# Twelve loads for a head pair instead of seventeen, the scale on the queries, and a new order for every engine

## The chip, the cores and the metric

The kernel runs on one core of a Trainium2 chip. The metric is the time of one execution on the device, in microseconds (us).

## The reference

Two attention stages follow each other; all numbers are float32.

```python
# stage 1: q, k, v are [8 batches, 8 heads, 576 tokens, 64]
scores = q @ k.T / 8
keep   = scores >= max(scores, axis=-1) - tau          # tau = 0.02
attn   = exp(where(keep, scores, -1e9) - max) ; attn /= sum(attn) + 1e-9
x      = heads side by side of (attn @ v)              # [8, 576, 512]
# stage 2: four experts e of width 64, the two best of a token by its gate logits
logits = x @ w_gate                                    # [512, 4]
q, k, v = x @ wq[e], x @ wk[e], x @ wv[e]
ye     = softmax(causal(q @ k.T / 8)) @ v @ wo[e]
out   += (share of e in the token's two best) * ye     # [8, 576, 512]
```

## The kernel before

The work of stage 1 is cut into 32 **pairs**: two heads of one batch, numbered n. Pair n loads its queries, keys and values, turns queries and keys by TensorE transposes (tasks `tq.n`, `tk.n`), moves the turned tiles from PSUM to SBUF (the pairs 0 to 3 as plain float32, the later ones split into a high and a low part), and then makes five score tiles of 128 tokens or 64 (`scores`, tiles in the order 4, 2, 3, 0, 1). A score tile of one head costs VectorE two passes over 128x576: `s_min`, which moves the scores and finds the largest, and `s_stt`, which sets the threshold and sums. ScalarE makes the exponential between the two. A scaling by the reciprocal (`scale2`) may run on GpSimd, VectorE or ScalarE. Then TensorE transposes the weights (`turned`) and multiplies them with the values (`attnv`, the matmuls `pm`, `pt`, `pe` times `vm`, `vt`). After each fourth pair the second stage of that batch (`second`) follows: projections, gate, causal scores, values, output, store. Weights are split once into high and low parts at the start (`weights`).

All of it is a list of some 5,000 tasks. Nothing is scheduled on the chip: the table `ORDER` gives each task its place in one overall sequence, and the table `BY` gives the engine of each task that more than one engine can do. `plan` walks through the sequence with a cost for each task; from these costs it picks the PSUM banks and SBUF slots, and puts fillers (matmuls on `tri` whose result nobody reads) into the start. Each engine then runs its own tasks in the order in which they stand, and waits at each for what it needs. SyncE (SP) issues the loads and stores in its order too: a load that waits for its buffer holds up those behind it.

`ki` and `qi`, the tiles into which keys and queries are loaded, exist once (`SLOTS`), so a pair's keys can only be loaded when the transposes of the pair ahead have read them; `vm` and `vt` exist twice. For a pair the kernel issues 17 loads: six for the keys (`KEYS`), five for the queries (`QUERIES`), two of 128 KB for the values and four for the last 64 tokens of the values (`vt`). Every piece of keys or values is one token's row of 64 numbers, 256 bytes. The keys are scaled by -1/8 (`qsc`, made from `tau`) as they leave PSUM.

GpSimd and VectorE share a path to SBUF. `plan` held two lists of spans (`mine`, `theirs`) from which the function `hit` works out an expected delay, and `told` puts each GpSimd task behind the last VectorE pass of this kind.

Of the kernel before, what the change touches and what calls it, by code (L numbers as in the profile page):

```python
# [44 lines left out]
KEYS = tuple((j, *x) for j in range(2) for x in ((SM, 1, 0, 0), (0, 4, 1, 0), (WH - ST, 5, 0, 1)))  # L45
# [57 lines left out]
JIT = 50.0  # L103
# [7 lines left out]
class Space:  # L111
# [47 lines left out]

def plan(tasks, filler, told=None):  # L160
# [6 lines left out]
    mine, theirs, holder = [], [], None  # L167
    order = []
    for t in sorted(tasks, key=lambda t: t.place):
# [30 lines left out]
        if t.port and e == "DVE":  # L200
            more = sum(hit(start, a, z - 200.0) for a, z in theirs[-6:])
            mine.append((start, start + more + lat - 177.0))
            at["POOL"] += sum(hit(a, *mine[-1]) for a, z in theirs[-6:] if a > start)
        elif e == "POOL":
            more = sum(hit(start, a, z) for a, z in mine[-8:])
            theirs.append((start + more, start + more + lat))
            at["DVE"] += sum(hit(a, theirs[-1][0], theirs[-1][1] - 200.0) for a, z in mine[-8:] if a > start)
# [45 lines left out]
SMALL = (172, 80)  # L253


def work(K):
# [20 lines left out]
    def dma(fn, deps, takes=(), uses=(), move=576.0, name="", e="SP"):  # L277
        late = 0.0 if isinstance(e, str) else 500.0
# [41 lines left out]
    def load(n):  # L320
        ki, qi, vm = (Buf(x) for x in ("ki", "qi", "vm"))
        e = "SP" if n else ("SP", "ACT")
        into = lambda *a: (lambda: K.load_in(*a)) if n else lambda e: K.load_in(*a, e)
        dk = [dma(into(K.kis, K.k, n, *x, ki), (), [ki], move=72.0 * x[2], name=f"ldk.{n}", e=e) for x in KEYS]
        dq = [dma(into(K.qis, K.q, n, *x, qi), (), [qi], move=72.0 * x[2], name=f"ldq.{n}", e=e) for x in QUERIES]
        dv = [dma(lambda j=j: K.load_v(n, vm, j), (), [vm], name=f"ldv.{n}") for j in range(2)]
        dv += [dma(lambda j=j, x=x: K.load_vt(n, vm, j, x), (), [vm], move=72.0, name=f"ldv.{n}") for j in range(2) for x in range(2)]
# [3 lines left out]
    def prep(n):  # L331
        ki, qi, dk, dq, dv = LD[n]
        PREP[n] = []
        for cls, src, tiles, d, scale, f in (("kk", ki, K.kis, dk, True, "k"), ("qq", qi, K.qis, dq, False, "q")):
            buf, g = Buf(cls), Buf("d")
            if not n:
                o = []
                for y in range(2):
                    m = pe((R + 1) * TR + TX, lambda g=g, src=src, tiles=tiles, y=y: K.tr_in(g, tiles, src, (y,)), [z for z, a in zip(d, KEYS if scale else QUERIES) if a[-1] == y], [g], [src], "R", ld=76.0, kind="T", name=f"t{f}.{n}")
# [23 lines left out]
    def scores(n, s):  # L363
# [13 lines left out]
        ms = [task("DVE", (782, 80), lambda j=j: K.s_min(bufs[j], scs[j], sm, j), [a], [sc, sm], [bufs[j], sc, sm], name=f"min.{n}.{s}") for j in range(nj)]  # L377
# [4 lines left out]
        for j in range(nj):  # L382
            x = task("DVE", (831, 77), lambda j=j: K.s_stt(scs[j], sm, ees[j], j), [es[j], th], [], [sc, sm, ee], name=f"stt.{n}.{s}")
# [34 lines left out]
    def weights(c):  # L418
# [7 lines left out]
        gb = Buf("sm")  # L426
        d = dma(lambda: K.load_g(c, gb), (), [gb], move=72.0, name="w")
        h = task("POOL", (204, 30), lambda: K.g_hi(c, gb), [d], [], [gb], name="w")
        WT.append(task("POOL", (206, 30), lambda: K.g_lo(c, gb), [h], [], [gb], name="w"))
# [132 lines left out]
    TAU.append(dma(K.load_tau, (), move=8.0, name="tau", e=("SP", "ACT")))  # L562
# [4 lines left out]
    for n in range(NPR):  # L567
        load(n)
        prep(n)
# [29 lines left out]
    "ldk": [
# [8 lines left out]
    ],  # L608
    "ldq": [
# [7 lines left out]
    ],  # L617
    "ldv": [
# [1023 lines left out]
```

## Time and profile before

| what | value |
|---|---|
| median of three runs | 799.91 us (798.96 to 800.9) |
| the profiled execution, own time | 800.27 us |
| span of its instructions | 798.5 us |
| TensorE busy | 774.9 us (97% of the span) |
| VectorE busy | 714.1 us (89%) |
| ScalarE busy | 680.3 us (85%) |
| GpSimd busy | 378.2 us (47%) |
| granted TensorE clock | 1.0 of full speed |

The span runs from the first instruction to the last; the execution's own time is 1.77 us more. Matmuls overlap in TensorE, so a busy share of 97% says that there was nearly always one in flight, not that none waited.

### The profile page before, as it was taken

How to read it: one execution, taken by the hardware profiler on the slowest of the kernel's cores; microseconds unless marked ns; L12 is line 12 of the kernel's file. 1: busy time of each engine (PE TensorE's matmuls, PEld its weight loads, DVE VectorE, ACT ScalarE, POOL GpSimd, SP SyncE). 2: the span in 40 equal slices, each digit the busy share in tenths (PEclk: the TensorE clock that was granted, in tenths of full speed). 3: DMA queues.
4: the chain of work that ended last, by engine and by line, in shares of the span. 5: the costliest groups of instructions: out<-in, count | busy, mean ns of one | idle time of the engine just before them, and what ended most of it. 6: DMA issues, size and time to landing. Idle time of an engine off the chain costs nothing.

```text
span 798.5 us, 34332 instructions
## 1 busy us (share of the span) xinstructions
PE 774.9 (97%) x14047; PEld 724.3 (91%) x14047; DVE 714.1 (89%) x2271; ACT 680.3 (85%) x1294; POOL 378.2 (47%) x766
## 2 busy tenths in 40 slices
PE   9889999999999999999999999999999999999997
PEld 6677998899989999898999999999998999988997
DVE  6999989998999889999999988999999989999483
ACT  5999989988899789887899869999789987999474
POOL 3577445434554435634466435464264623456231
PEclk9999999999999999999999999999999999999999
DMA  4343211122122122222121222213222122210002
GB/s 112 82 90 87 60 36 29 45 51 73 36 67 71 35 54 55 50 65 68 41 73 35 70 70 50 47 23 75 54 47 52 42 73 66 56 31 12 9 28 95
DMA packets 140237, 44.19 MB, mean 55 GB/s; under 512 B 135216, under 2 KB 135216, under 8 KB 140080
## 3 DMA queue, kind: packets, MB, share of 16 engines
q1 hardware_dynamic: 138640, 41.65, 21.4%
q8 instruction: 111, 1.82, 1.0%
q10 hardware_dynamic: 1440, 0.34, 0.2%
q14 instruction: 46, 0.38, 0.2%
HBM read 32.51 MB, written 9.44 MB: 53 GB/s over the span
## 4 chain that ended last, share of the span: by engine, by line
PE 72%; DVE 11%; ACT 8%; SPq 3%; issue 2%; DMA 2%; POOL 1%; ACTq 0%; DVEq 0%
PE ps L1142 59%; PE ps L1276 10%; DVE e L992 8%; SPq L1145 3%; PE ps L1132 3%; ACT pm L1118 2%; ACT e L1255 2%; DMA qi<-in_q_dram 1%; ACT e L1530 1%; POOL e L992 1%; DVE sm L992 1%; ACT pt L1118 1%; ACT e L1551 0%; DVE z L992 0%; DMA ki<-in_k_dram 0%
## 5 line engine op out<-in xcount | busy, mean ns | idle before, releaser
L992 POOL TENSOR_SCALAR e<-e,sm 128x576 f32<-128x576 f32 (+4 forms) x289 | 196.1, 688 | 94.7 <-DVE sm L992 51.6
L992 DVE TENSOR_SCALAR_CACHE_REDUCE e<-ps 128x576 f32<-128x576 f32 x288 | 209.1, 751 | 19.1 <-PE ps L1142 12.9
L1255 ACT ACTIVATE e<-e,sm 128x576 f32<-128x576 f32 x288 | 212.5, 770 | 8.2 <-DVE e L992 7.4
L992 DVE SCALAR_TENSOR_TENSOR e<-e,sm,e 128x576 f32<-128x576 f32 x256 | 205.6, 828 | 7.2 <-POOL sm L992 2.7
L1142 PE MATMUL ps<-kk,qq 64*128 64x288 f32 x1840 | 175.0, 313 | 3.6 <-DVE e L992 1.0
L1142 PEld LDWEIGHTS ps<-kk,qq 64*128 64x128 f32 x1840 | 136.9, 185 | 15.5 <-DVE e L992 3.2
L1118 ACT ACTIVATE pm<-ps 128x1024 f32<-128x1024 f32 (+1 forms) x142 | 140.4, 1002 | 6.9 <-PE ps L1276 5.0
L1142 PE MATMUL ps<-pm,vm 128*64 128x128 f32 x2048 | 120.1, 273 | 0.0
L1276 PE MATMUL ps<-ident,e 64*128 64x64 f32 x2624 | 114.1, 225 | 5.8 <-POOL e L992 1.3
L1276 PEld LDWEIGHTS ps<-ident,e 64*128 64x128 f32 x2624 | 102.6, 138 | 15.1 <-POOL e L992 3.5
L1142 PEld LDWEIGHTS ps<-pm,vm 128*64 128x64 f32 x2048 | 111.1, 137 | 1.2 <-ACT pm L1118 0.4
L1142 PE MATMUL ps<-x,wh 64*128 64x288 f32 x1024 | 106.5, 294 | 0.0
L992 POOL TENSOR_TENSOR sm<-sm 128x2 f32<-128x2 f32 (+1 forms) x132 | 26.7, 208 | 137.7 <-DVE e L992 108.1
L1142 PEld LDWEIGHTS ps<-x,wh 64*128 64x128 f32 x1024 | 88.9, 185 | 0.3 <-issue 0.2
L1551 ACT ACTIVATE e<-e,sm 128x576 f32<-128x576 f32 (+4 forms) x113 | 80.2, 726 | 6.6 <-DVE sm L992 6.2
L1142 PE MATMUL ps<-x,wl 64*128 64x288 f32 x512 | 83.5, 292 | 0.0
L1530 ACT ACTIVATE e<-e,sm 128x384 f32<-128x384 f32 (+3 forms) x128 | 70.6, 555 | 4.8 <-DVE sm L992 4.6
L1142 PE MATMUL ps<-wh,x 64*128 64x260 f32 x576 | 60.5, 282 | 0.0
L992 DVE CUSTOM_DVE_ANT_0 e<-ps,tri 128x384 f32<-128x384 f32 (+3 forms) x128 | 58.6, 484 | 1.9 <-PE ps L1142 1.0
L1142 PE MATMUL ps<-woh,z 64*128 64x256 f32 x512 | 57.9, 289 | 1.1 <-DVE zt L992 0.4
L1142 PEld LDWEIGHTS ps<-x,wl 64*128 64x128 f32 x512 | 56.8, 184 | 0.0
L1118 ACT ACTIVATE rw<-ps 128x576 f32<-128x576 f32 (+1 forms) x57 | 36.8, 646 | 22.9 <-PE ps L1142 17.5
(151 smaller groups left out, 1498.2 us busy)
## 6 DMA issues: line engine op xcount, KB each, us to landing
vm<-in_v_dram SPq DMA_DIRECT2D x64, 128.0 KB, 2.5
out_dram<-ob SPq DMA_DIRECT2D x32, 256.0 KB, 2.2
ki<-in_k_dram SPq DMA_DIRECT2D x63, 80.0 KB, 2.4
qi<-in_q_dram SPq DMA_DIRECT2D x62, 80.0 KB, 2.4
ki<-in_k_dram SPq DMA_DIRECT2D x63, 64.0 KB, 2.3
qi<-in_q_dram SPq DMA_DIRECT2D x32, 64.0 KB, 2.3
vt<-in_v_dram SPq DMA_DIRECT2D x128, 16.0 KB, 2.2
qi<-in_q_dram SPq DMA_DIRECT2D x32, 48.0 KB, 2.4
```

The source lines that it names most:

```text
L992: self.made.append(f(*args, **kw))
L1118: self.nc.scalar.activation(dst, src, AF.Copy)
L1132: self.nc.tensor.transpose(self.ps[:, bank, c * n:(c + 1) * n], x[sl], self.ident[sl, sl])
L1142: return self.nc.tensor.matmul(out, x, y, start=first, stop=last)
L1145: (self.nc.sync if e == "SP" else self.nc.scalar).dma_start(dst, src)
L1255: self.nc.scalar.activation(self.row(e), self.row(sc), AF.Exp, bias=self.small(sm)[:, 2 * j:2 * j + 1], scale=-1.0)
L1276: self.nc.tensor.transpose(self.ps[:, g.slot + h, c * D:(c + 1) * D], x, self.ident[sl, sl])
L1530: self.nc.scalar.activation(p, p, AF.Exp, bias=m[:, 2 * j:2 * j + 1], scale=-1.0, accum_out=m[:, 4 + 2 * j:5 + 2 * j])
L1551: self.nc.scalar.activation(p, p, AF.Copy, scale=x)
```

## The change

A pair's keys arrive with two transfers of 128 KB, one for each head, in which every partition gets four tokens that lie one behind the other (1 KB), and two transfers of 16 KB each for half of the tile that holds the last 64 tokens of both heads. The values arrive the same way with one transfer of 256 KB for both heads, and their last 64 tokens with two transfers instead of four. The queries keep their five. The order of the keys within a head thereby changes, for keys and values alike. The scale moves from the keys to the queries: keys are copied out of PSUM, in pieces of 64 columns, and queries are multiplied by `qsc`. The gate's weights come in one transfer instead of four, with two GpSimd tasks instead of eight. The weights' loads wait for those of pair 0. In `plan` the expected delay on the shared path is replaced by a plain rule (a VectorE pass of this kind starts when GpSimd is done), and three VectorE costs are lowered. `ORDER` and `BY` are written anew.

```diff
-KEYS = tuple((j, *x) for j in range(2) for x in ((SM, 1, 0, 0), (0, 4, 1, 0), (WH - ST, 5, 0, 1)))
+KEYS = tuple((x, tail) for tail in range(2) for x in range(2))
...
         if t.port and e == "DVE":
-            more = sum(hit(start, a, z - 200.0) for a, z in theirs[-6:])
-            mine.append((start, start + more + lat - 177.0))
-            at["POOL"] += sum(hit(a, *mine[-1]) for a, z in theirs[-6:] if a > start)
+            start = max(start, busy - 200.0)
         elif e == "POOL":
...
+            busy = start + lat
...
-SMALL = (172, 80)
+SMALL = (158, 80)
...
-        dv = [dma(lambda j=j: K.load_v(n, vm, j), (), [vm], name=f"ldv.{n}") for j in range(2)]
-        dv += [dma(lambda j=j, x=x: K.load_vt(n, vm, j, x), (), [vm], move=72.0, name=f"ldv.{n}") for j in range(2) for x in range(2)]
+        dv = [dma(lambda: K.load_v(n, vm), (), [vm], move=1152.0, name=f"ldv.{n}")]
+        dv += [dma(lambda x=x: K.load_vt(n, vm, x), (), [vm], move=144.0, name=f"ldv.{n}") for x in range(2)]
...
-        for cls, src, tiles, d, scale, f in (("kk", ki, K.kis, dk, True, "k"), ("qq", qi, K.qis, dq, False, "q")):
+        for cls, src, tiles, d, scale, f in (("kk", ki, K.kis, dk, False, "k"), ("qq", qi, K.qis, dq, True, "q")):
...
-        ms = [task("DVE", (782, 80), lambda j=j: K.s_min(bufs[j], scs[j], sm, j), [a], [sc, sm], [bufs[j], sc, sm], name=f"min.{n}.{s}") for j in range(nj)]
+        ms = [task("DVE", (757, 80), lambda j=j: K.s_min(bufs[j], scs[j], sm, j), [a], [sc, sm], [bufs[j], sc, sm], name=f"min.{n}.{s}") for j in range(nj)]
...
-            x = task("DVE", (831, 77), lambda j=j: K.s_stt(scs[j], sm, ees[j], j), [es[j], th], [], [sc, sm, ee], name=f"stt.{n}.{s}")
+            x = task("DVE", (818, 77), lambda j=j: K.s_stt(scs[j], sm, ees[j], j), [es[j], th], [], [sc, sm, ee], name=f"stt.{n}.{s}")
...
+                if t.move and t.name == "w":
+                    t.after += [*LD[0][2], *LD[0][3]]
...
     "tau": [
-        1, 18, 2,
+        1, 2, 3,
     ],
...
+    def load_k(self, n, x, tail, ki, e="SP"):
+
+        t, k = self.kis[ki.slot], self.heads_of(self.k, n)
+        if tail:
+            self.dma(t[HEADS[x], R], k[:, SM:].rearrange("j p d -> p j d"), e)
+        else:
+            self.dma(t[:, :R, x], k[x, :SM].rearrange("(p c) d -> p c d", c=R), e)
...
+    def load_v(self, n, vm):
+        self.dma(self.vms[vm.slot].rearrange("p j c d -> p j (c d)"), self.heads_of(self.v, n)[:, :SM].rearrange("j (p c) d -> p j (c d)", c=R))
...
+    def blocks(self, x):
+        return x.rearrange("p (c h q) -> p h c q", h=2, q=D)
```

On SP, at the start of the program, the first loads stood so before (`ki` and `qi` are keys and queries, `ob` the weights on their way, `vt` the last values):

```order
L1145 DMA tau_t<-in_tau_dram 128x1
L1145 DMA ki_76<-in_k_dram 64x4x64
L1145 DMA qi_77<-in_q_dram 64x3x64
L1145 DMA ki_76<-in_k_dram 64x5x64
L1145 DMA ki_76<-in_k_dram 64x64
L1145 DMA qi_77<-in_q_dram 64x4x64
L1145 DMA ob_3_195<-in_moe_wo_dram 128x512
L1145 DMA ob_4_198<-in_moe_wo_dram 128x512
```

and now they stand so:

```order
L1125 DMA ki_76<-in_k_dram 128x4x64
L1125 DMA tau_t<-in_tau_dram 128x1
L1125 DMA qi_77<-in_q_dram 64x5x64 x2
L1125 DMA qi_77<-in_q_dram 64x4x64
L1125 DMA ob_2_174<-in_moe_wq_dram 128x4x64
L1125 DMA ob_4_198<-in_moe_wq_dram 128x4x64
```

The first pair's share of SP went from five loads and `tau` to four and `tau`; ScalarE's own queue issued six loads of that pair before its first computation, and now five.

On TensorE, near the end of the program, the last transposes and the last product with the values stood so before (`woh` and `wol` are the output weights, `z` and `zt` what they multiply, `zt` the last 64 tokens; `pm`, `pt` times `v` is the product with the values):

```order
L1132 MATMUL ps<-ident,e_908_16402 128x64 x12
L1132 MATMUL ps<-ident,e_907_16399 128x64 x8
L1142 MATMUL ps<-woh,zt_858_15431 128x256 x2
L1142 MATMUL ps<-wol,zt_858_15431 128x256 x2
...
L1142 MATMUL ps<-wol,z_927_16817 128x256 x2
L1142 MATMUL ps<-woh,z_927_16817 128x256 x2
L1132 MATMUL ps<-ident,e_924_16776 128x64 x8
L1132 MATMUL ps<-ident,e_929_16879 128x64 x4
L1142 MATMUL ps<-pm_930_16897,v_90 64x128 x6
```

and now they stand so:

```order
L1112 MATMUL ps<-ident,e_916_16459 128x64 x4
L1112 MATMUL ps<-ident,e_922_16531 128x64 x12
L1112 MATMUL ps<-ident,e_924_16591 128x64 x8
L1122 MATMUL ps<-pm_930_16679,v_90 64x128 x6
...
L1122 MATMUL ps<-woh,z_931_16718 128x256 x2
L1122 MATMUL ps<-woh,zt_865_15372 128x256 x2
L1122 MATMUL ps<-wol,zt_865_15372 128x256 x2
L1122 MATMUL ps<-woh,zt_865_15372 128x256 x4
```

Two runs of transposes became one, and the second half of the output of `zt`, which stood ahead of the last product, now stands behind it, between two pieces of the output of `z`.

## Rows read from the trace of the kernel before

**Rows 1.** The page's head: span, then busy time, share and instructions by engine.

```profile
span 798.5 us, 34332 instructions
...
PE 774.9 (97%) x14047; PEld 724.3 (91%) x14047; DVE 714.1 (89%) x2271; ACT 680.3 (85%) x1294; POOL 378.2 (47%) x766
```

**Rows 2.** Busy time by stretch: length, PE, PEld, DVE, ACT, POOL; clock, DMA, GB/s.

```profile
20.00:40.00 20.00, 17.63 (x259) 13.71 (x257) 18.65 (x59) 18.98 (x31) 10.06 (x20) 1.00 0.38 82
40.00:60.00 20.00, 17.50 (x306) 14.66 (x304) 19.17 (x53) 18.62 (x31) 14.25 (x27) 1.00 0.41 91
60.00:80.00 20.00, 18.39 (x324) 15.31 (x320) 19.92 (x60) 18.45 (x29) 14.55 (x27) 1.00 0.38 86
```

**Rows 3.** PE's waits, whole span: us in total, times, longest us.

```profile
PE ps L1276 <- DMA qi<-in_q_dram: 2.8, 3, 1.0
PE ps L1276 <- ACT pm L1118: 2.2, 3, 1.5
...
PE ps L1142 <- ACT pe L1118: 0.9, 2, 0.6
...
PE ps L1276 <- DMA ki<-in_k_dram: 0.3, 1, 0.3
```

**Rows 4.** The chain that ended last, first 12 us: start, us, what.

```profile
3.71 0.60 ACTq L1145
...
4.35 2.97 DMA ki<-in_k_dram
...
8.51 3.63 PE ps L1142 x25
```

**Rows 5.** PE's timeline, 782 to 799: start us, us, instructions, wait before.

```profile
783.13 0.78 PE L1132 MATMUL ps<-ident,e 64*128 64x64 f32 x20
783.73 0.36 PE L1142 MATMUL ps<-woh,zt 64*128 64x256 f32 x2
783.93 0.28 PE L1142 MATMUL ps<-wol,zt 64*128 64x256 f32 x2
784.05 0.40 PE L1142 MATMUL ps<-woh,zt 64*128 64x256 f32 x4
...
785.24 0.57 PE L1132 MATMUL ps<-ident,e 64*128 64x64 f32 x12
785.74 0.88 PE L1142 MATMUL ps<-pm,v 128*64 128x128 f32 x12
786.45 0.82 PE L1142 MATMUL ps<-pt,v 128*64 128x128 f32 x12
787.10 0.82 PE L1142 MATMUL ps<-pm,v 128*64 128x128 f32 x12
787.76 0.82 PE L1142 MATMUL ps<-pt,v 128*64 128x128 f32 x12
788.51 0.39 PE L1142 MATMUL ps<-woh,z 64*128 64x256 f32 x2
788.73 0.28 PE L1142 MATMUL ps<-wol,z 64*128 64x256 f32 x2
...
789.21 0.28 PE L1142 MATMUL ps<-woh,z 64*128 64x256 f32 x2
789.77 0.38 PE L1142 MATMUL ps<-woh,z 64*128 64x256 f32 x2 [0.28 <-DVE z L992]
```

**Rows 6.** DMA issues on SP, line L1145: duration ns min/median/max, first and last start.

```profile
L1145 SPq DMA_DIRECT2D ki<-in_k_dram x189: 465/611/1721, 1.2 to 697.6; - x189
```

**Rows 7.** DMA issues: count, KB of one, median us from issue to landing.

```profile
vt<-in_v_dram SPq DMA_DIRECT2D x128, 16.0 KB, 2.2
...
ob<-in_moe_wo_dram SPq DMA_DIRECT2D x2, 256.0 KB, 3.1
```

**Rows 8.** Groups by line and shape: count, busy us, mean ns, idle before.

```profile
L992 DVE TENSOR_REDUCE sm<-sm 128x2 f32<-128x4 f32 x157 | 22.9, 150 | 3.4 <-ACT e L1530 2.0
...
L992 DVE TENSOR_TENSOR x<-rw,x 128x288 fp32r<-128x288 f32 x18 | 8.4, 465 | 0.0
...
L1551 ACT ACTIVATE e<-e,sm 128x576 f32<-128x576 f32 (+4 forms) x113 | 80.2, 726 | 6.6 <-DVE sm L992 6.2
```

More of the change, by code (lines that the diff above doesn't have):

```diff
@@ L133, in take @@
         where = range(GLOW, 8) if b.cls == "g" else range(0, 8, 2) if b.cls == "s" else range(6, -1, -2) if b.cls == "d" else range(SLOTS[b.cls])
-        ok = [i for i in where if self.at(b, i) + lag <= now]
+        now_ = now + 1e-6
+        ok = [i for i in where if self.at(b, i) + lag <= now_]
         if not ok:
@@ L137, in take @@
         elif b.cls == "g":
-            b.slot = max(ok, key=lambda i: (self.banks[i ^ 1] + lag > now, i))
+            b.slot = max(ok, key=lambda i: (self.banks[i ^ 1] + lag > now_, i))
         else:
@@ L166, in plan @@
     moved = 0.0
-    mine, theirs, holder = [], [], None
+    holder, busy = None, 0.0
     order = []
@@ L275, in pe, with dma @@
         return x
-    def dma(fn, deps, takes=(), uses=(), move=576.0, name="", e="SP"):
-        late = 0.0 if isinstance(e, str) else 500.0
+    def dma(fn, deps, takes=(), uses=(), move=576.0, name="", e="SP", late=0.0):
+        late += 0.0 if isinstance(e, str) else 500.0
         t = (2000.0 + late + move, 1335.0 + late + move)
@@ L338, in prep @@
                 for y in range(2):
-                    m = pe((R + 1) * TR + TX, lambda g=g, src=src, tiles=tiles, y=y: K.tr_in(g, tiles, src, (y,)), [z for z, a in zip(d, KEYS if scale else QUERIES) if a[-1] == y], [g], [src], "R", ld=76.0, kind="T", name=f"t{f}.{n}")
+                    m = pe((R + 1) * TR + TX, lambda g=g, src=src, tiles=tiles, y=y: K.tr_in(g, tiles, src, (y,)), [*d[:2], d[3 - y]] if f == "k" else [z for z, a in zip(d, QUERIES) if a[-1] == y], [g], [src], "R", ld=76.0, kind="T", name=f"t{f}.{n}")
                     h = evac(WH + 80 * scale, lambda e, g=g, buf=buf, scale=scale, y=y: K.in_hi(e, buf, g, scale, (y,), n < NF), [m, *WARM, *(TAU[1:2] if scale else ())], [buf], [g, buf], name=f"{f}h.{n}")
@@ L425, in weights @@
             WT.extend([h, minus(256, lambda e, w=w, st=st: K.w_lo(e, c, w, st), [h], [st], "wl")])
[L426 to L429, printed above, removed]
+        if not c:
+            gb = Buf("ob")
+            d = dma(lambda: K.load_g(gb), (), [gb], move=200.0, name="w")
+            h = task("POOL", (214, 30), lambda: K.g_hi(gb), [d], [], [gb], name="w")
+            WT.append(task("POOL", (230, 30), lambda: K.g_lo(gb), [h], [], [gb], name="w"))
         if c < EP:
@@ L561, in work @@
     WARM.append(task("ACT", (1460, 110), K.warm, (), name="warm"))
-    TAU.append(dma(K.load_tau, (), move=8.0, name="tau", e=("SP", "ACT")))
+    TAU.append(dma(K.load_tau, (), move=8.0, name="tau", e=("SP", "ACT"), late=900.0))
     TAU.append(task("DVE", SMALL, K.key_scale, TAU[:1], name="tau"))
@@ L568, in work @@
         load(n)
+        if not n:
+            for t in tasks:
+                if t.move and t.name == "w":
+                    t.after += [*LD[0][2], *LD[0][3]]
         prep(n)
@@ new lines @@
+    "xr": "00000000100010000100000000000000",
+    "xh": "01010010000100010000100100010000",
+    "xl": "0011111101100001000011010000000100000000010001000100010001010011",
+    "xd": "00000110001111000100000100000000",
+    "kr": "00100",
+    "qr": "00000",
+    "fpj": "03133033130133332333230233313213",
+    "qu": "00000001000100100000000000000001",
+    "ql": "0000000001000001100100000000101010000000000001000000100001000001010011000000000100000010001111",
+    "qd": "02212100120001010110020011011001",
@@ L978 @@
+    "fo": "333311131332033113333333303213321221",
+    "ob": "000000000000000000000000100100000100",
+    "kl": "100000000000000000000000000000",
 }
@@ L1145, in dma, with heads_of @@
         (self.nc.sync if e == "SP" else self.nc.scalar).dma_start(dst, src)
-    def load_in(self, tiles, src, n, j, row, nb, c, h, buf, e="SP"):
+    def heads_of(self, src, n):
         b, hp = divmod(n, NPAIR)
-        rows = src[b, 2 * hp + j, row:row + nb * D, :]
-        self.dma(tiles[buf.slot][h * D:(h + 1) * D, c:c + nb, j], rows.rearrange("(c p) d -> p c d", p=D), e)
-    def load_v(self, n, vm, j):
-        b, hp = divmod(n, NPAIR)
-        self.dma(self.vms[vm.slot][:, j], self.v[b, 2 * hp + j, :SM, :].rearrange("(r p) d -> p r d", r=R))
@@ new lines, in load_q, with load_vt @@
+    def load_q(self, n, j, row, nb, c, h, qi, e="SP"):
+        b, hp = divmod(n, NPAIR)
+        rows = self.q[b, 2 * hp + j, row:row + nb * D, :]
+        self.dma(self.qis[qi.slot][h * D:(h + 1) * D, c:c + nb, j], rows.rearrange("(c p) d -> p c d", p=D), e)
+    def load_v(self, n, vm):
+        self.dma(self.vms[vm.slot].rearrange("p j c d -> p j (c d)"), self.heads_of(self.v, n)[:, :SM].rearrange("j (p c) d -> p j (c d)", c=R))
+    def load_vt(self, n, vm, x):
+        t = self.vts[vm.slot][HEADS[x]].rearrange("p j x d -> p (j x) d")
+        self.dma(t[:, 1:3] if x else t[:, 0:4:3], self.heads_of(self.v, n)[:, SM:].rearrange("j p d -> p j d"))
@@ L1163, in tr_in @@
     def tr_in(self, g, tiles, buf, hs=(0, 1)):
+        x = tiles[buf.slot].rearrange("p c j d -> p c (j d)")
         for c in range(R + 1):
-            x = tiles[buf.slot][:, c].rearrange("p j d -> p (j d)")
-            for h in hs:
-                self.turn(g, c, x[HEADS[h]], h)
+            for y in hs:
+                h = 1 - y if tiles is self.kis else y
+                w = x[HEADS[h], (c + h * R) % (R + 1) if tiles is self.kis else c]
+                self.turn(g, c, w, h, y)
     def kq(self, buf):
@@ L1307, in av @@
                 o, w = ((R * (j ^ s // 2) + c) * P, P) if s < R else (c * P + j * ST, ST)
[L1308 removed]
+                self.mm(out[j * D:(j + 1) * D], v[:, j, c] if c < R else vt[:, j, 1], pt.ap[:, o:o + w], self.opens(g, bank, j), False)
     def opens(self, g, bank, j):
```

212 lines of the change are left out of this document (95 added, 117 removed), and 358 rows, old and new, of the table ORDER.

## The prediction

> **What bounds the kernel now.** The page's head comes first [rows 1]: TensorE has a matmul in flight for 774.9 of 798.5 us. No matmul is added or removed by the change, but for one filler (80 instead of 79), so the time can only move by what stands between the matmuls: 23.6 us without any, and what is lost inside the busy time when TensorE changes from one kind of work to another. The view by stretches shows where the idle time is thickest [rows 2]: from 20 to 80 us TensorE is busy for 53.5 of 60 us, and there VectorE is busy for 57.7 (19.92 of 20 in the last third) and ScalarE for 56.1. In this stretch there is only first-stage work, and VectorE feeds it. The list of TensorE's waits then says for whom it waits [rows 3]: 2.8 us for loaded queries, 0.3 us for loaded keys, 3.1 us for two kinds of copies by ScalarE (2.2 and 0.9), the rest in small pieces. So the loads, which the change treats most visibly, cost 3.1 us at the place where it counts, whatever SP does all day. The chain of the first 12 us shows one more place [rows 4]: the last keys of pair 0 are issued by ScalarE's queue, land 2.97 us after 4.35, at 7.3 us, and the first scores start at 8.51. TensorE's timeline near the end shows the price of changing work [rows 5].
>
> **The change, part by part.**
>
> *Fewer loads.* An issue takes SP 0.611 us [rows 6], and 162 fewer DMAs stand on SP (437 instead of 599, all kinds counted), which frees 99 us of SP. That is not the gain: SP mostly waits for buffers. What counts is how early the last load of a pair lands after `ki` and `qi` are free. Five fewer issues for a pair are 3.1 us of queue, when all stand behind each other. The longest wait for a load is 1.0 us [rows 3], so each is covered even when only two of the five come out ahead of the awaited one. The bounds are 0 (the awaited load stands behind a store or another wait as before) and -3.1 us. I take **-2.5 us**, near the upper end, since two places fewer suffice.
>
> Landing could cost something back: a value load of 256 KB now has to land whole. The nearest rows are 3.1 us for 256 KB and 2.2 us for 16 KB [rows 7], so at most 0.9 us for a buffer that exists twice and is filled far ahead. I count 0; without that cover it would be 0.9 us a pair for some of the 32 pairs, which the range's upper part has to hold.
>
> By the Trainium skill ("DMA: Bandwidth & Descriptors", Specifications) a piece under 512 B does not run at the line rate, and keys and values go from pieces of 256 B to 1 KB. By that rule alone all load waits would end, and the sum below would be 0.6 us lower, at 794.9; the landing rows, 0.9 us apart for 16 times the bytes, say that the bytes matter little, and I keep the row.
>
> *The start.* ScalarE's queue issues five loads instead of six and SP four with `tau` instead of five with it. One issue less is 0.60 us on the queue that ended last [rows 4]. The second keys are no longer behind the others on that queue, which allows at most 1.2 us (two issues); the copies between transposes and scores stay. I take **-0.8 us**, with 0 to -1.2. It is carried on, because what follows is bound by VectorE, which starts earlier too.
>
> *The order on TensorE.* I counted its runs in both orders. Transposes stand in 189 runs before and in 173 now. Products with values (tiles 128\*64 and 64\*64, taken together) stand in 65 runs before and in 60 now. The price comes from starts in the timeline [rows 5]. Twenty transposes take from 783.13 to 783.73, 0.60 us, or 0.06 a pair. The first pair of output matmuls behind them takes 0.20 us (783.73 to 783.93), the next one 0.12 (to 784.05): a run of transposes costs 0.08 us beyond its own work. For a run of products: twelve transposes ahead of it take 0.50 instead of 0.36 (+0.14), the first twelve products 0.71 against 0.65 and 0.66 for the next two groups (+0.06), the last twelve 0.75 (+0.10), and the first output pair 0.22 instead of 0.12 (+0.10): together 0.40 us. Nine of the 16 runs that vanish stood behind whole-row matmuls (151 such entries, now 142): 9 x 0.08 = 0.7 us. The other seven stood behind products, and their exit is already in the 0.40. Five runs of products fewer: 5 x 0.40 = 2.0 us. Together **-2.7 us**. Where VectorE sets the pace, a switch saved only makes TensorE wait longer, so the weak bound is 0.
>
> By the Trainium skill ("TensorEngine Tiling (Array Packing)", Key Properties) a change of tiling mode drains TensorE. By that rule a change from 64\*128 transposes to 64\*128 matmuls, one mode, would be free, and the sum would be 0.7 us higher, at 796.2; the 0.20 us against 0.12 of the row speaks against leaving it out.
>
> *The tail.* At 789.21 the output of `z` stops for 0.56 us instead of 0.12, waiting for the second half of `z` [rows 5]. Now the second output of `zt` stands there, which waits for nothing new: **-0.4 us**, with 0 to -0.4.
>
> *Scale and pieces of 64 columns.* Keys lose the multiplication and queries gain it, with the same tile sizes on the same engines (26 splits of either on VectorE before and now). They change places, so 0. Reading PSUM in 64-column pieces is what all turned tiles already do.
>
> *VectorE's load.* It gets 18 more instructions (1,715 instead of 1,697), most of them short: 14 more sums of pairs at 0.15 us and 12 more shares, against fewer small splits. What counts is the stretch to 80 us, where it has no idle time to give [rows 2]. Ahead of the first split of queries straight from PSUM (pair 6, behind 45 `s_min` passes in both orders) there now stand 163 instructions instead of 153. The additions there are nine sums (9 x 0.15 = 1.35) and three splits of 128x288 (3 x 0.465 = 1.4) [rows 8]; what left is of the size of one long pass. I take **+2.0 us**, between 0 (ScalarE or the loads were late there anyway) and +4 (all additions and none of the removals, with one more `s_stt`).
>
> *GpSimd's scalings.* Seventeen of 128x576 leave GpSimd, and 14 more stand on ScalarE, 0.726 us each [rows 8]. ScalarE is idle for 15% of the span, so I count 0; uncovered it is the slow rival below.
>
> *Sum:* -2.5 - 0.8 - 2.7 - 0.4 + 2.0 = -4.4 us. The profiled execution took 800.27 us, of which 798.5 are the span; 800.27 - 4.4 = 795.87. The median of the runs is 0.36 us below the profiled one, so the prediction is **795.5 us**. All good ends together give -7.6 (792.3), all weak ones +4 (803.9).
>
> **Rivals.**
>
> *VectorE swallows it (no change).* If the first 80 us run at VectorE's pace throughout, the earlier loads buy nothing there and half of the saved switches are lost: -0.8 - 1.35 - 0.4 + 2.0 = -0.55, or 799.4 us. For it speaks 19.92 of 20 us in the last third of the stretch; against it that TensorE's waits name loads and ScalarE, and that most runs that vanish lie later.
>
> *ScalarE becomes the late one (slower).* The 14 added scalings stand in ScalarE's order beside the copies that TensorE already waits for (3.1 us, [rows 3]). If each delays such a copy by its length, 14 x 0.726 = 10.2 us come on top: 805.7 us. From 6.0 us on, 59% of it, the kernel is slower by more than 0.2%. For it speaks that ScalarE is busy for 56.1 of 60 us where the time is lost; against it 118 us of idle time in all.
>
> *The new order also closes the other gaps (faster still).* From 20 to 80 us TensorE is idle for 6.5 us [rows 2]. If the freed SP queue and the new order halve that beyond what is counted, 3.2 us go: 792.3 us.
>
> **How the numbers follow.** A measurement of this kernel can tell about 0.2% (1.6 us) from no change. The forecast's case, 793 to 798.3, has 0.44; the faster rival, below 793, 0.22; no change, 798.3 to 801.5, 0.16; slower, 0.18. So faster is 0.66, same 0.16, slower 0.18. The range that leaves out no more than 2 in 10 is 788 to 804: its upper end is the sum of all weak ends, its lower end 4 us under the sum of all good ones, for gaps in the middle that the new order may close and that I have no row for. The forecast's own range is 793 to 798.3.
>
> **What would show it.** SP issues about 437 DMAs; TensorE's waits for `qi` and `ki` fall from 3.1 us to under 1; the first scores start near 7.7 us; TensorE's busy time falls by 2 to 3 us, as switches are inside it; the stretch from 20 to 80 us keeps VectorE at 19 of 20 or more. Wrong would be: waits for `pm` or `pe` copies on ScalarE well over 3.1 us, or new waits for VectorE in the middle of the program, which this order may open at places that no row of before shows.

## The result, and the profile after

| | before | changed |
|---|---|---|
| median of four runs each, side by side | 800.4 us (798.96 to 802.28) | **792.1 us** (791.52 to 792.63) |
| ratio, 95% interval | | 0.9893 [0.9866, 0.992] |
| the profiled execution | 800.27 us | 791.85 us |
| span | 798.5 us | 790.1 us |

The kernel became 8.3 us faster, 6.4 to 10.7 by the interval. The forecast was 795.5, with 793 to 798.3 as its own range and 788 to 804 as the wide one; the time lies in the range of the rival "the new order also closes the other gaps" (below 793).

The page's head after, which answers to [rows 1]:

```profile
span 790.1 us, 34160 instructions
...
PE 772.0 (98%) x14048; PEld 723.0 (92%) x14048; DVE 711.8 (90%) x2289; ACT 683.3 (86%) x1300; POOL 369.4 (47%) x736
```

TensorE's busy time fell by 2.9 us, and its time without a matmul from 23.6 to 18.1 us (790.1 - 772.0), by 5.5. The stretches of [rows 2] read now:

```profile
20.00:40.00 20.00, 19.43 (x302) 15.51 (x298) 19.97 (x64) 20.00 (x36) 9.85 (x22) 1.00 0.40 93
40.00:60.00 20.00, 19.07 (x298) 15.61 (x298) 19.96 (x68) 19.88 (x33) 10.66 (x19) 1.00 0.44 103
60.00:80.00 20.00, 19.34 (x389) 17.61 (x391) 19.81 (x61) 19.87 (x32) 8.28 (x15) 1.00 0.35 88
```

From 20 to 80 us TensorE is busy for 57.8 us instead of 53.5, VectorE for 59.7 instead of 57.7, ScalarE for 59.7 instead of 56.1, and GpSimd for 28.8 instead of 38.9. The waits of TensorE that answer to [rows 3]:

```profile
PE ps L1277 <- ACT pm L1098: 0.8, 3, 0.3
...
PE ps L1277 <- DMA ki<-in_k_dram: 0.7, 1, 0.7
...
PE ps L1277 <- ACT pe L1098: 0.2, 1, 0.2
PE ps L1277 <- DMA qi<-in_q_dram: 0.2, 1, 0.2
```

Loads keep TensorE waiting for 0.9 us instead of 3.1, and the ScalarE copies of [rows 3] for 1.0 instead of 3.1. The chain of the first 12 us, as [rows 4], passes through no landing of a load any more (from 1.52 to 5.97 us it runs through TensorE's fillers, and only behind the scores, from 11.58 us, through SP's issuing of loads); the first scores start at 7.36 instead of 8.51:

```profile
1.52 4.45 PE ps L1122 x20
5.96 0.57 PE ps L1277 x12
...
6.79 0.53 ACT qq L1180
...
7.36 4.22 PE ps L1122 x29
```

And in TensorE's timeline near the end, as [rows 5], the output of `z` is followed after 0.12 us by that of `zt`, where TensorE stood for 0.56:

```profile
781.22 0.28 PE L1122 MATMUL ps<-woh,z 64*128 64x256 f32 x2
781.34 0.28 PE L1122 MATMUL ps<-woh,zt 64*128 64x256 f32 x2
```

**Where the front's time came from.** The best place to compare is the start of VectorE's 37th `s_stt` pass of this form: 90.15 us before, 84.90 after, 5.3 us earlier. Up to there VectorE has made the same 45 `s_min` and 36 `s_stt` passes (of the other form of `s_stt`, without a second `e`, five before and four after), and TensorE has been busy for nearly the same time. First before, by groups of VectorE from 0 to 90.2 us, then by stretch with all engines:

```profile
L992 DVE TENSOR_SCALAR_CACHE_REDUCE e<-ps 128x576 f32<-128x576 f32 x45 | 32.4, 748 | 2.8 <-PE ps L1142 2.7
L992 DVE SCALAR_TENSOR_TENSOR e<-e,sm,e 128x576 f32<-128x576 f32 x37 | 31.8, 884 | 0.1
L992 DVE SCALAR_TENSOR_TENSOR e<-e,sm 128x576 f32<-128x576 f32 x5 | 4.3, 852 | 0.0
...
L992 DVE TENSOR_TENSOR wl<-ob,wh 128x256 fp32r<-128x256 f32 x4 | 2.5, 616 | 0.0
```

```profile
0.00:90.20 90.20, 80.89 (x1213) 66.11 (x1215) 80.31 (x235) 77.09 (x122) 50.38 (x114) 1.00 0.40 90
```

The same two views after, from 0 to 84.9 us:

```profile
L972 DVE TENSOR_SCALAR_CACHE_REDUCE e<-ps 128x576 f32<-128x576 f32 x45 | 32.2, 749 | 0.4 <-PE ps L1122 0.4
L972 DVE SCALAR_TENSOR_TENSOR e<-e,sm,e 128x576 f32<-128x576 f32 x37 | 29.3, 831 | 0.1
...
L972 DVE SCALAR_TENSOR_TENSOR e<-e,sm 128x576 f32<-128x576 f32 x4 | 3.2, 810 | 0.0
...
L972 DVE TENSOR_TENSOR wl<-ob,wh 128x256 fp32r<-128x256 f32 x4 | 1.7, 431 | 1.4 <-ACT wh L1098 1.4
```

```profile
0.00:84.90 84.90, 80.63 (x1222) 66.85 (x1222) 77.19 (x245) 76.26 (x127) 42.40 (x98) 1.00 0.42 100
```

VectorE has ten instructions more behind it (245 against 235), as the prediction had counted for the queries of pair 6 (163 against 153), and yet is 3.1 us *less* busy: its passes are shorter. The means of `s_stt` in the two views, 884 and 831 ns, still hold the 37th pass (0.80 us before, 1.24 after); the 36 ahead of it take 886 and 820 ns. The low parts of the weights take 431 instead of 616. These two alone are 36 x 66 ns + 4 x 185 ns = 3.1 us. Summed over all of VectorE's instructions up to the 37th pass, by what each adds to the busy time, the instructions that came and went are worth +2.1 us at the durations of before, and the changed durations -5.2: -2.5 in `s_stt`, -1.3 in low parts (of the weights and of `x`), and most of the rest in short sums and reciprocals that now follow another instruction without a pause. GpSimd was busy for 8 us less beside them. VectorE's idle time fell by another 2.2 us (9.9 to 7.7), and `s_min`'s wait for TensorE from 2.8 to 0.4.

How a pass becomes longer shows in the timeline of before around 38 us, VectorE and GpSimd in turn:

```profile
37.83 1.97 POOL L992 TENSOR_SCALAR e<-e,sm 128x576 f32<-128x576 f32 x2 [0.77 <-DVE e L992]
37.97 1.21 DVE L992 SCALAR_TENSOR_TENSOR e<-e,sm,e 128x576 f32<-128x576 f32 x1
...
39.11 1.29 DVE L992 SCALAR_TENSOR_TENSOR e<-e,sm,e 128x576 f32<-128x576 f32 x1
39.76 1.23 POOL L992 TENSOR_TENSOR wl<-ob,wh 128x256 fp32r<-128x256 f32 x1
```

Two passes run beside GpSimd's scalings, the second then beside a low part of the weights, and take 1.21 and 1.29 us. Sorted so over the first 100 us, the `s_stt` passes of before (both forms) that overlap no GpSimd work take 811 ns on the mean (25 of them, 797 to 821), those that overlap some 966 (20, the longest 1351); after, 810 (38) and 888 (10). Above 811 ns that is 3.1 us before and 0.8 after. In the whole of either execution, no pass that has GpSimd idle beside it takes more than 823 ns. The Trainium skill ("SBUF — State Buffer", Who interferes with whom) states that a VectorE instruction with two inputs in SBUF contends with a GpSimd instruction that reads SBUF; `s_stt` has two, and these rows agree.

### The profile page after: what moved, and what is told of

The parts are those of the page before. It is cut to its first block, busy times and chain, and to the rows that moved or that the text cites. A ratio compares the mean times of both kernels' runs of the same rounds, so it can differ in the third digit from the quotient of the medians.

```text
span 790.1 us, 34160 instructions
## 1 busy us (share of the span) xinstructions
PE 772.0 (98%) x14048; PEld 723.0 (92%) x14048; DVE 711.8 (90%) x2289; ACT 683.3 (86%) x1300; POOL 369.4 (47%) x736
## 4 chain that ended last, share of the span: by engine, by line
PE 71%; DVE 16%; ACT 7%; issue 3%; DMA 1%; POOL 1%; SPq 1%; DVEq 0%; ACTq 0%; POOLq 0%
PE ps L1122 59%; DVE e L972 12%; PE ps L1277 9%; PE ps L1112 2%; ACT pm L1098 1%; DVE sm L972 1%; ACT e L1256 1%; ACT e L1534 1%; DMA ki<-in_k_dram 1%; ACT e L1555 1%; DMA qi<-in_q_dram 1%; ACT pt L1098 1%; DVE qq L972 1%; SPq L1125 1%; POOL e L972 0%
## 5 line engine op out<-in xcount | busy, mean ns | idle before, releaser
L1256 ACT ACTIVATE e<-e,sm 128x576 f32<-128x576 f32 x288 | 213.8, 771 | 14.5 <-DVE e L972 13.8
L972 POOL TENSOR_SCALAR e<-e,sm 128x576 f32<-128x576 f32 (+4 forms) x271 | 183.8, 688 | 86.3 <-DVE sm L972 58.3
L1122 PE MATMUL ps<-kk,qq 64*128 64x288 f32 x1840 | 172.1, 312 | 2.0 <-ACT pt L1098 0.7
L1122 PE MATMUL ps<-pm,vm 128*64 128x128 f32 x2048 | 121.8, 274 | 0.0
L1277 PEld LDWEIGHTS ps<-ident,e 64*128 64x128 f32 x2624 | 100.9, 138 | 15.2 <-DVE e L972 3.5
L1555 ACT ACTIVATE e<-e,sm 128x576 f32<-128x576 f32 (+4 forms) x132 | 92.7, 720 | 7.0 <-DVE sm L972 5.6
L1534 ACT ACTIVATE e<-e,sm 128x256 f32<-128x256 f32 (+3 forms) x128 | 70.8, 557 | 1.6 <-DVE sm L972 1.2
L1098 ACT ACTIVATE rw<-ps 128x576 f32<-128x576 f32 (+1 forms) x59 | 38.4, 651 | 29.5 <-PE ps L1122 28.9
L972 DVE CUSTOM_DVE_ANT_0 e<-ps,tri 128x512 f32<-128x512 f32 (+3 forms) x128 | 58.0, 486 | 4.0 <-PE ps L1122 2.4
L972 POOL TENSOR_TENSOR x<-rw,x 128x288 fp32r<-128x288 f32 (+1 forms) x67 | 43.4, 660 | 33.9 <-DVE sm L972 15.4
L1122 PE MATMUL ps<-woh,z 64*128 64x256 f32 x512 | 55.8, 286 | 0.0
```

The costliest lines, as they stand in the source:

```text
L972: self.made.append(f(*args, **kw))
L1098: self.nc.scalar.activation(dst, src, AF.Copy)
L1122: return self.nc.tensor.matmul(out, x, y, start=first, stop=last)
L1256: self.nc.scalar.activation(self.row(e), self.row(sc), AF.Exp, bias=self.small(sm)[:, 2 * j:2 * j + 1], scale=-1.0)
L1277: self.nc.tensor.transpose(self.ps[:, g.slot + (h if bank is None else bank), c * D:(c + 1) * D], x, self.ident[sl, sl])
L1534: self.nc.scalar.activation(p, p, AF.Exp, bias=m[:, 2 * j:2 * j + 1], scale=-1.0, accum_out=m[:, 4 + 2 * j:5 + 2 * j])
```

## The experiments

Every kernel was timed beside the kernel before; the table gives its median less that one's, so that the changed kernel stands at -8.3. The medians of before were 800.08 us for the first four, 799.99 for the next four and 799.29 for the last four. The intervals are about 1 us to either side, and 2.2 us for the changed kernel, which ran four times: in the last column, less than about 2 us says little.

| kernel | median us | ratio [95%] | against before | against the changed kernel |
|---|---|---|---|---|
| changed | 792.1 | 0.9893 [0.9866, 0.992] | -8.3 | |
| new_list_17 | 809.54 | 1.0115 [1.0098, 1.0131] | +9.5 | +17.8 |
| old_list_12 | 804.93 | 1.0064 [1.0049, 1.0079] | +4.9 | +13.2 |
| sums_on_pool | 793.1 | 0.9915 [0.9902, 0.9928] | -7.0 | +1.3 |
| runs_split | 809.81 | 1.0123 [1.011, 1.0136] | +9.7 | +18.0 |
| merged_only | 798.1 | 0.9983 [0.9973, 0.9992] | -1.9 | +6.4 |
| split_1_to_6 | 797.43 | 0.9976 [0.9966, 0.9987] | -2.6 | +5.7 |
| split_from_7 | 800.45 | 1.001 [0.9998, 1.0022] | +0.5 | +8.8 |
| pieces_256 | 791.73 | 0.9903 [0.9889, 0.9918] | -8.3 | 0.0 |
| extra_ahead | 801.95 | 1.0031 [1.0021, 1.0042] | +2.7 | +11.0 |
| extra_inside | 804.36 | 1.006 [1.0044, 1.0075] | +5.1 | +13.4 |
| extra_dve | 799.39 | 1.0005 [0.9995, 1.0016] | +0.1 | +8.4 |
| extra_act | 797.16 | 0.9972 [0.9962, 0.9982] | -2.1 | +6.2 |

**The new order with 17 loads** (`new_list_17`).

```diff
-            self.dma(t[:, :R, x], k[x, :SM].rearrange("(p c) d -> p c d", c=R), e)
+            src = k[x, :SM].rearrange("(p c) d -> p c d", c=R)
+            for sl in HEADS:
+                self.dma(t[sl, :R, x], src[sl], e)
...
+        for j in range(2):
+            self.dma(self.vms[vm.slot].rearrange("p j c d -> p j (c d)")[:, j], src[:, j])
```

> The changed kernel with its order, but 17 transfers for a pair again: each head's keys in two transfers (halves of the partitions), the values in two (one a head), their tails in four. The pieces stay 1 KB. Theory 'list' (most of the 8.3 us comes from the new order, which keeps VectorE and ScalarE filled in the first 80 us): the time stays within 1.6 us of the changed kernel's 792.1, so at most 793.7. Theory 'loads' (the order can only fill them because loads come in time): at least 4 us are given back, 796 or more, TensorE's waits for qi and ki go back to 3 us, and VectorE's busy time from 20 to 80 us falls below 58.5 of 60 us. Between the two, both have a share.

It is 17.8 us slower than the changed kernel and slower than the kernel before. TensorE's waits:

```profile
PE ps L1282 <- DMA ki<-in_k_dram: 6.2, 12, 1.2
PE ps L1282 <- DMA qi<-in_q_dram: 3.7, 4, 2.4
PE ps L1122 <- SPq L1419: 2.6, 4, 1.0
```

Five issues more bring the waits for loads to 9.9 us, three times those of before, and VectorE's busy time from 20 to 80 us falls to 54.9 us: theory "loads" held, and "list" fell. The third line is TensorE waiting for SP itself: a matmul that is cut in two has a semaphore instruction between its parts, which SP may carry (`fence`), and that stands in SP's queue behind the loads. So with 17 loads this order is worse than the one before.

**The order of before with 12 loads** (`old_list_12`). The code and the planner's costs are those of after, `ORDER` and `BY` those of before, where twelve of the 17 places are kept.

```diff
-    "ldk": [4, 0, 5, 7, 55, 52, 47, 54, ...
+    "ldk": [4, 7, 8, 10, 32, 59, 68, 75, ...
```

> The changed kernel's code (12 transfers, scale on queries, its planner costs) with the order and engines of the kernel before; of its 17 places for a pair's loads the earliest four of the keys, one of the values and two of the tails are kept; the gate's weights come in four transfers as before. Theory 'list': at most 2.5 us better than before, 797.5 or more. Theory 'loads': most of the gain is there without the new order, 795 or less, and TensorE's busy time from 20 to 80 us rises from 53.5 towards 57.8 us.

It is 4.9 us slower than before, though TensorE waits for loads for 1.4 us only. Its stretch from 40 to 60 us has TensorE busy for 16.1 us, less than before (17.5):

```profile
40.00:60.00 20.00, 16.08 (x282) 13.26 (x282) 18.64 (x53) 18.33 (x30) 13.33 (x27) 1.00 0.36 90
```

Theory "loads" fell: TensorE is busy for 52.3 of the 60 us from 20 to 80. But here the planner's slots and fillers were chosen from other costs than the order was written for, which may be what cost the time (this was not tried alone), so it says little about the loads; hence the next one.

**The kernel before with 12 loads and nothing else** (`merged_only`): its order, its planner, its slots. Five of the 17 tasks issue nothing, and the scale is on the queries.

```diff
-        dv = [dma(lambda j=j: K.load_v(n, vm, j), (), [vm], name=f"ldv.{n}") for j in range(2)]
+        dv = [dma(lambda j=j: None if j else K.load_v(n, vm), (), [vm], name=f"ldv.{n}") for j in range(2)]
```

> The kernel before, with its order, engines, planner and slots, but 12 transfers for a pair: five of the 17 load tasks issue nothing, and the others issue the new, larger transfers (for pair 0 both heads' keys, which the first transposes now need, stand earlier). The scale is on the queries, as the new tile layout wants. Theory 'loads alone' (my -2.5 us and -0.8 us): 795 to 798 beside 800. Theory 'only together' (new_list_17 and old_list_12 are both slower than before: the order is made for its loads): within 1.6 us of before, 798.5 to 801.7; slower than that would say that the larger transfers, which must land whole, come too late for the old order.

It is 1.9 us faster than before (1.4 by the ratio, 0.6 to 2.2 by its interval). The loads by themselves, with the scale, are worth that, of the 8.3: 798.1 lies just between the ranges of the two theories. Its profiled execution took 800.5 us, the longest of its eleven, and shows what a late load at the start can cost. The timeline of TensorE, then its stretches with the granted clock:

```profile
7.53 0.71 PE L1303 MATMUL ps<-ident,ki 64*128 64x64 f32 x5 [1.32 <-DMA ki<-in_k_dram]
...
9.63 3.19 PE L1142 MATMUL ps<-kk,qq 64*128 64x288 f32 x11
```

```profile
6.00:8.00 2.00, 0.68 (x9) 0.92 0.96 317
8.00:10.00 2.00, 2.00 (x16) 0.50 0.11 23
10.00:12.00 2.00, 2.00 (x11) 0.50 0.20 47
12.00:14.00 2.00, 2.00 (x11) 0.50 0.12 27
14.00:16.00 2.00, 2.00 (x16) 0.87 0.58 130
```

Behind a wait of 1.32 us, in a stretch in which TensorE is busy for 0.68 of 2 us, the granted clock is 0.50, that is 1.2 instead of 2.4 GHz, until past 14 us, and eleven score matmuls take 3.19 us where twelve took 1.73 in the changed kernel. A wait alone need not do that: behind one of 1.47 us (the kernel before, at 28.5 us) and one of 1.87 us (`split_from_7` below, at 176.9 us) the clock stays at 1.00:

```profile
28.00:34.00 6.00, 5.50 (x72) 3.98 (x74) 4.77 (x14) 5.01 (x9) 1.06 (x4) 1.00 0.43 97
```

```profile
176.00:182.00 6.00, 5.08 (x79) 4.94 (x81) 4.47 (x15) 4.10 (x6) 1.62 (x3) 1.00 0.07 17
```

**Loads split by pairs** (`split_1_to_6`, `split_from_7`): the 17 loads of `new_list_17` for the pairs 1 to 6 alone, or from pair 7 on.

```diff
-        for j in range(2):
+        for j in ([0, 1] if 1 <= n <= 6 else [slice(0, 2)]):
```

> The changed kernel with 17 transfers again for the pairs 1 to 6 alone; pair 0 and the later ones keep 12. Theory 'front' (SP's queue is the tight place only while the first pairs are loaded one behind the other): 5 to 9 us slower than 792.1, so 797 to 801, with the loss complete by 100 us. Rival (the 17 us of new_list_17 came evenly, or from pair 0): under 3 us slower.

> The changed kernel with 17 transfers again from pair 7 on. Theory 'front': under 3 us slower, at most 795. Rival (SP's queue is tight throughout, since it also carries the fences between the two halves of crossed matmuls, and TensorE waits for these): 6 us or more slower, 798 or more, with TensorE's waits for SP's fences near 1.6 us and for ki and qi near 5 us.

They cost 5.7 and 8.8 us, together 14.5 of 17.8; if the parts add up, the remaining 3.3 are left for pair 0 and what it delays: in `new_list_17` its queries come 0.38 and 0.30 us late, the next pair's keys 1.25 us in three waits, and behind these the granted clock is 0.50 from 16 to 18 us. (It is so again from 186 to 189 us, behind a wait of 2.42 us.) Theory "front" was right on the first six pairs, 0.95 us a pair, with 5.3 us lost at the 37th `s_stt` pass (90.2 us), and fell on the others, which it took to be nearly free: the 25 pairs behind cost 0.35 us each. In the profiled execution of `split_from_7`, the fastest of its twelve, the waits for loads are 5.3 us, near the 5 of its rival; those for SP's fences are 0.6, not 1.6:

```profile
PE ps L1285 <- DMA qi<-in_q_dram: 2.7, 2, 1.9
PE ps L1285 <- DMA ki<-in_k_dram: 2.6, 4, 1.0
```

**Pieces of 256 bytes** (`pieces_256`): few issues, but one token to a piece; the values in one transfer a head, so 13 loads.

```diff
-            self.dma(t[:, :R, x], k[x, :SM].rearrange("(p c) d -> p c d", c=R), e)
+            self.dma(t[:, :R, x], k[x, :SM].rearrange("(c p) d -> p c d", c=R), e)
```

> The changed kernel with keys and values in pieces of 256 bytes again (tokens 128 apart on a partition), 13 transfers a pair, the values one a head. Theory 'count' (the number of issues on SP decides, not the pieces): at most 1.6 us slower, 793.7, and less than 0.3 us more from issue to landing. Rival 'pieces' (1 KB pieces land much sooner): 3 us or more slower, 795 or more.

No difference. The keys land in the same time (median, last number of a line); first after, then this kernel:

```profile
ki<-in_k_dram SPq DMA_DIRECT2D x63, 128.0 KB, 2.7
```

```profile
ki<-in_k_dram SPq DMA_DIRECT2D x63, 128.0 KB, 2.6
```

Theory "count" held: in this kernel the number of issues counts, and not the length of the pieces.

**Ten small sums on GpSimd** (`sums_on_pool`): ten sums of the first six pairs (five of `thr`, as shown, and five of `eps1`), 0.15 us each, from VectorE to GpSimd.

```diff
-    "thr": "1110022212210000010001200021220202201220 ...
+    "thr": "1112022212212020210201220021220202201220 ...
```

> The changed kernel with 10 of the 28 small sums (threshold and denominator) that VectorE makes in the first six pairs given back to GpSimd, as many as it had before (28 of 60). Theory 'sums' (the new front is full because VectorE no longer waits for GpSimd's sums): 2 to 5 us slower than the changed kernel, 794 to 797, and VectorE idle from 20 to 80 us rises from 0.3 to over 2 us. Rival (it is the order of the passes, or the loads): within 1 us of 792.1, the sums hide behind other passes.

1.3 us slower, which the two intervals leave open; at the 37th `s_stt` pass it is 0.9 us behind (85.76 against 84.90), as much as a wait of TensorE for queries at 16.6 us that the changed kernel does not have. Theory "sums" fell: VectorE is idle from 20 to 80 us for 0.3 us, as in the changed kernel. VectorE saves nothing by the ten sums: up to the 37th `s_stt` pass it makes ten instructions fewer and is busy for 77.20 us, in the changed kernel for 77.19. GpSimd is busy for 1.8 us more beside it, and the passes are longer again, the 37 `s_stt` at 839 ns (831 in the changed kernel) and the low parts of the weights at 528 (431):

```profile
0.00:85.76 85.76, 80.18 (x1220) 66.56 (x1222) 77.20 (x235) 76.26 (x126) 44.18 (x107) 1.00 0.42 98
```

```profile
L972 DVE SCALAR_TENSOR_TENSOR e<-e,sm,e 128x576 f32<-128x576 f32 x37 | 29.6, 839 | 0.1
...
L972 DVE TENSOR_TENSOR wl<-ob,wh 128x256 fp32r<-128x256 f32 x4 | 2.1, 528 | 1.7 <-ACT wh L1098 1.7
```

**VectorE's and ScalarE's share in the front** (`extra_dve`, `extra_act`): one `s_min` pass, or one `s_exp` pass, done twice for ten score tiles of the pairs 1 to 5.

```diff
-        ms = [task("DVE", (757, 80), lambda j=j: K.s_min(bufs[j], scs[j], sm, j), ...
+        ms = [task("DVE", (757, 80), lambda j=j: [K.s_min(bufs[j], scs[j], sm, j) for _ in range(2 if 1 <= n <= 5 and s in (0, 2) and not j else 1)], ...
```

> The changed kernel with one of its s_min passes on VectorE done twice for 10 score tiles in pairs 1 to 5 (10 x about 0.7 us = 7 us more on VectorE in the first 90 us; the same result is written twice). Theory 'VectorE sets the pace of the front': 5 to 7.5 us slower than the changed kernel, 797 to 799.5. Rival 'VectorE is covered there, though it is busy for 19.9 of 20 us': at most 1.5 us slower.

> The changed kernel with one of its s_exp passes on ScalarE done twice for the same 10 score tiles (10 x 0.77 = 7.7 us more on ScalarE in the first 90 us; the same result is written twice). Theory 'VectorE alone sets the pace of the front': at most 1.5 us slower than the changed kernel. Rival 'ScalarE sets it as well, at 19.9 of 20 us in the new order': 5 to 7.5 us slower, 797 to 799.5.

Both cost what they add: 8.4 us for 7.1 us of VectorE (718.9 busy against 711.8), and 6.2 for 6.6 us of ScalarE. The sums of the stretch from 20 to 80 us, of the changed kernel, of `extra_dve` and of `extra_act`:

```profile
sum 60.00, PE 57.84 PEld 48.72 DVE 59.74 ACT 59.74 POOL 28.79; mean PE 19.28 PEld 16.24 DVE 19.91 ACT 19.91 POOL 9.60
```

```profile
sum 60.00, PE 53.87 PEld 43.92 DVE 59.69 ACT 56.19 POOL 27.81; mean PE 17.96 PEld 14.64 DVE 19.90 ACT 18.73 POOL 9.27
```

```profile
sum 60.00, PE 54.67 PEld 44.65 DVE 56.83 ACT 59.79 POOL 28.52; mean PE 18.22 PEld 14.88 DVE 18.94 ACT 19.93 POOL 9.51
```

So the front runs at the pace of VectorE and ScalarE, both without slack in the new order; the theory that VectorE alone sets it fell. A microsecond more on either moves the end by about one. That one less would bring as much is not shown.

**The price of a run of transposes** (`runs_split`, `extra_ahead`, `extra_inside`). The first moves 32 whole-row matmuls into runs of transposes that followed them, so that 205 runs stand where there were 173:

```diff
-    "s": [..., 2458, ...
+    "s": [..., 2451.5, ...
```

> The changed kernel with 32 runs of transposes cut in two, all behind the first 100 us: a piece of whole-row matmuls that stood behind the run now stands in its middle. My price of 0.08 us for such a run gives +2.6 us, 794.7, and TensorE's busy time rises by as much. Rival (TensorE waits anyway where they stand, so a cut is free): within 0.8 us of 792.1. Well over 3 us would say that the later transposes delay what waits for them.

18.0 us, or 0.56 a cut: too much to be the switch. TensorE's busy time rises by 7.9 us and its time without a matmul by 9.7; its waits for copies of `pm` rise from 1.0 to 5.9 us, presumably because the later half of a run comes later to those who need it. What the 7.9 us of busy time consist of is not shown, so this run gives no price for a cut. The other two add 76 pairs of plain matmuls with 64 columns, ahead of a run of transposes or inside the same run:

```diff
+    def extra(self):
+        if self.left:
+            self.left -= 1
+            if not self.left:
+                g, c = self.where
+                for h, sl in enumerate(HEADS):
+                    self.mm(self.ps[:, g.slot + h, c * D:(c + 1) * D], self.ident[sl], self.ident[sl, :D], True, True)
```

> The changed kernel with an extra pair of plain fp32 matmuls (identity by 64 columns of the identity, overwritten by the transposes that follow) ahead of 76 runs of transposes that stand behind whole-row matmuls. It leaves nothing out. 76 pairs of 64 columns in fp32 by about 0.11 us (the later output pairs of the timeline take 0.12) are 8 to 9 us of TensorE's time, and no run of transposes is cut. Theory 'switch' (a run of transposes costs 0.08 us beyond its work): 792 + 9 = 801, and the next kernel, with the same pairs inside the runs, is 76 x 0.08 = 6.1 us above this one. Rival 'free' (the exit from transposes costs nothing, or TensorE's waits take it up): the two stand within 1.5 us of each other.

> The same 76 pairs, in the middle of the same runs of transposes, so that 76 runs more of transposes begin and end; consumers get their data at the same place as in extra_ahead. Theory 'switch': 6.1 us above extra_ahead (76 x 0.08), about 807, with as much more busy time on TensorE. Rival 'free': within 1.5 us of extra_ahead.

A pair costs 0.145 us (11.0 / 76), and 2.4 us more where it cuts a run: 0.03 us a run, between the two theories. TensorE's busy time, which leaves out a wait of 1.7 us for queries that `extra_inside` alone shows, says the same, 783.4 and 785.9 us:

```profile
PE 783.4 (98%) x14352; PEld 736.7 (92%) x14352; DVE 713.7 (89%) x2289; ACT 685.3 (86%) x1300; POOL 368.0 (46%) x736
```

```profile
PE 785.9 (98%) x14352; PEld 739.4 (92%) x14352; DVE 714.3 (89%) x2289; ACT 685.5 (85%) x1300; POOL 368.2 (46%) x736
```

## Why the prediction was right in its direction, and which step failed

The profiled executions differ by 8.4 us (800.27 - 791.85), where the sum was -4.4. At the 37th `s_stt` pass 5.3 us are won, and the other 3.1 come later. This cuts the prediction's terms in two groups (of the waits for loads, 1.0 us lies at 372 us and so behind the cut, but the whole term stands in the first row):

| terms | predicted | came |
|---|---|---|
| up to 85 us: loads -2.5, start -0.8, VectorE's load +2.0 | -1.3 | -5.3 (VectorE's busy time -3.1, its idle time -2.2) |
| behind it: TensorE's order -2.7, the tail -0.4 | -3.1 | -3.1 (TensorE's busy time there -2.6) |

- **VectorE's load: the step that failed.** "I take +2.0 us" counted the instructions that the order adds, at the durations of [rows 8], and the count was right: ten more, worth +2.1 us at the durations of before. But the durations are no constants, and for their change the sum had no term. With 8 us less of GpSimd work beside them the same passes took less, the durations together came to -5.2 us, and VectorE needed 3.1 us less than before. The row that would have said so is not the mean of a group but its spread by what runs beside it: 811 ns alone, 966 beside GpSimd. "GpSimd's scalings", counted as 0, is the same miss seen from the other side: taking work off GpSimd was worth something, on VectorE. (The "small pieces" that [rows 3] leaves out also held 1.3 us in which TensorE waited for GpSimd's scalings.) That the front then shows VectorE's time in full, the ground of this term, holds: `extra_dve` cost 8.4 us for 7.1. That it is the smaller share of GpSimd that shortens the passes rests on the traces and on one run: in the kernels with the old order they take 886 ns from 10 to 90 us (before, `merged_only`, `old_list_12`), in those with the new one 830 and 820 (changed, `new_list_17`), and 856 in `sums_on_pool`, which gives ten sums back to GpSimd and changes nothing else. No run moved GpSimd's scalings alone, so how much of the 5.2 us is theirs stays open.
- **Loads -2.5 and start -0.8.** The waits for loads fell by 2.2 us, and the first scores came 1.15 us earlier where 0.8 was taken. VectorE's idle time up to the 37th pass, in which both end, fell by 2.2 instead of 3.3. With little else changed (`merged_only`) the loads give 1.9. In the new order they are worth 17.8, since that order leaves SP no room for 17: 5.7 in the pairs 1 to 6, 8.8 behind them.
- **Landing 0.** Right: 256 KB of values land in 3.0 us, and only 0.2 and 0.7 us of waits are for loads. (The two small transfers of a pair's keys are of 32 KB each, not of 16 as the change was described, and land in 2.3 us.) The rule of the Trainium skill on pieces under 512 B ("DMA: Bandwidth & Descriptors", Specifications) changes nothing here: 791.73 with 256 bytes, 792.1 with 1 KB.
- **TensorE's order -2.7.** The size came (-2.6 busy behind the front, -2.9 in all), but not as it was added up, so that it came is in part luck. A run of transposes costs 0.03 us and not 0.08, which makes 0.3 of the 0.7. The 2.0 for five runs of products were not tried alone, and where the rest of the 2.6 comes from stays open.
- **The tail -0.4** came as forecast, and so did the signs named for the rest: 435 DMAs on SP (437 forecast), waits for `qi` and `ki` under 1 us, TensorE's busy time 2.9 us lower, VectorE at 19.8 or more of 20 us.
- **Ends and rivals.** The good ends of the terms add up to -7.4 (792.5), not to -7.6. "VectorE swallows it" had the right bound, but VectorE gave time instead of taking it. "ScalarE becomes the late one" did not come: the copies' waits of 3.1 us fell to 1.0, though ScalarE has no slack left from 20 to 80 us (`extra_act`). The faster rival is the one that came. Its gap did close, 4.3 of TensorE's 6.5 idle us from 20 to 80 where it took half beyond what was counted. That its 792.3 meets the measured 792.1 is luck all the same: its sum still holds +2.0 for VectorE, and it did not name the shorter passes that filled the gap.

## What to carry to other kernels

An order and the number of loads it was written for belong together: taken alone the loads gave 1.9 us, the new order with 17 loads lost 9.5, and both together won 8.3, so neither half may be judged by itself. Before an instruction is costed at its group's mean, look at what runs beside it: a pass that grows by a fifth beside another engine is shortened by moving *that* engine's work, even where it seemed free, and work handed to that engine can come back as longer passes (`sums_on_pool`). Where an engine is busy for 19 of 20 us in a stretch, price added work there in full, and look for loads and semaphore instructions that share one queue.

## What the hardware showed unexpectedly

- In `new_list_17` TensorE waited for SP 2.6 us in all, up to 1.0 at once: a semaphore instruction of 17 ns behind loads of 0.6 us each.
- Behind a wait of 1.32 us at the start (`merged_only`) the granted clock was 0.50 from 8 us until past 14, and eleven score matmuls took 3.19 us where twelve took 1.73; behind waits of 1.47 and 1.87 us later in other kernels it stayed at 1.00.
- GpSimd work stretched VectorE's two-input passes from 811 to 966 ns on the mean, and ten sums of 0.15 us moved to GpSimd left VectorE as busy as before.
- Pieces of 256 bytes and of 1 KB land within 0.1 us of each other at 128 KB a transfer (2.6 and 2.7 us).
